# Fewer TensorE instructions in a fused attention and soft-MoE kernel: key pairs turned together, logits computed transposed

## The chip, the core and the metric

The kernel runs on one core of one Trainium2 chip. Five engines work side by side, each with its own queue of instructions: TensorE (PE; its weight loads are shown apart as PEld), VectorE (DVE), ScalarE (ACT), GpSimd (POOL) and SyncE (SP), which here only issues transfers. The metric is the device time of one execution, in microseconds. Three runs of the kernel before gave 298.43, 299.58 and 299.91 us, a median of 299.58.

## The reference

Two layers, one after the other. Attention with a soft cap, over 8 batches of 12 heads, 448 positions and 64 columns a head; its result, 3584 rows of 768, goes into a soft mixture of 8 experts with 4 slots each.

```python
scores = (q @ k.T) / 8
attn = softmax(cap * tanh(scores / cap))        # cap = 30
x = (attn @ v) as rows of 768                   # 12 heads beside each other

logits = x @ phi                                # 3584 x 32
d = softmax of logits over the rows             # dispatch
slot_input = d.T @ x                            # 32 x 768
slot_out[e] = relu(slot_input[e] @ w1[e]) @ w2[e]
c = softmax of logits over the slots            # combine
out = c @ slot_out                              # 3584 x 768
```

## The kernel before

**Quads.** Attention is worked off in 24 quads Q, each of four heads of one batch; three quads are a batch b (`NQB` = 3). Two heads lie side by side in the 128 rows of the array. For a quad, q comes by a casting transfer on GpSimd's queue (`load`, L394) and k by a plain one on SyncE's (`load_k`, L399); VectorE casts k to bf16 (`cast_k`, L403). TensorE turns both (`turn`, L474): 7 tiles of 128 positions times 2 heads, 14 transposes, each with 64 columns of the array, for q as for k. VectorE copies the result to `qT`, `kT` and `km` (`turned`, L480 to L489). The 14 score tiles of a quad go through a ring of PSUM banks (`qk_chunk`, L504 and L507) to ScalarE, which takes the tanh of each chunk (L517) and the exp of 8 tiles at once (L525); the exp of the other 6 is made by VectorE as a sum of four terms (`term`, L532). Then come the products with v (`pv`, L542), the division by the row sum (`norm`, L575 and L576), the turn of x (`x_turn`, L587) and its copy (L591).

**Logits and slots.** After the third quad of a batch, `logits` (L596, L600) multiplies x by phi with x as the weights of the array: 30 matmuls with 32 columns of result each, 128 positions in the partitions. ScalarE takes their exp, `E` (L618, 128 by 128). GpSimd copies the tail rows to `ediag` (L623) and writes `E` four times side by side to `e4` (L628). TensorE adds up `x` times `E` for the slots (`slot_sums`, L671 and L674), sums `e4` with ones for the dispatch's denominators (`e_norm`, L635; `zacc`, L641) and turns `e4` into `ET` (`e_turn`, L646; `e_turned`, L650), the weights of the last product. That is done in the stage for batches 0 to 5; for the last two, turn and copy stand among the output tiles (L990 to L996), and the sum of batch 6 in `z_last` (L805).

**The order.** No scheduler runs on the chip. A class `Plan` lists all steps of the attention stage with engine, duration, dependencies, a due time (`DUE`) and a hold (`HOLD`), plays them through with the durations of `COST`, and the order it gets is written out by hand (`EMIT`) into each engine's queue. Three PSUM banks are handed out by the same plan. The expert weights go along as 56 transfers (`W`): 24 parts of w1, then 32 half parts of w2. Five of the w2 parts stay in SBUF (`KEPT`, `w2b`); 27 are cast from memory to memory (`w2d`, L334).

**The tail.** When the attention's tiles are free, SyncE loads the 27 spilled parts (`w2t`, L859). Then come the last batch's logits and slots, layer 1 (`layer1`, L880), layer 2 (`layer2`, L913, first all parts of the left half of the columns, then all of the right), and 28 output tiles, each `ET` times `so`, scaled and stored (L936 to L1018).

## Time and profile before

| | |
|---|---|
| median of three runs | 299.58 us |
| the profiled execution | 297.8 us |
| its span, first to last instruction | 296.0 us |
| attention, first to last tanh or exp of scores | about 9.6 to 247 us |
| last batch, layer 1 and layer 2 | about 248 to 268 us |
| output tiles and stores | about 263 to 296 us |

A row of the grouped view reads: line, engine, operation, result <- operand, shapes and count, then busy time and mean duration of one in ns, then idle time of the engine just before these instructions and what ended it. "issue" as the releaser means that the engine waited for nothing that another engine or a transfer in the profile did. In a timeline row the two numbers in front are start and length in us, and the idle time before it stands in brackets. In a windows row each engine's busy time in the window stands with its count of instructions in brackets, then the clock granted to TensorE, the share of time in which the 16 DMA engines had packets (queues overlap, so it may exceed 1) and the rate in GB/s. Matmuls overlap: one of 219 ns may start 30 ns after the one before.

### The profile page before, as it was taken

What the parts mean: (1) busy time and instruction counts of PE and PEld (TensorE: products, weight loads), DVE (VectorE), ACT (ScalarE), POOL (GpSimd) and SP (SyncE); (2) the same over time, 40 slices, a digit from 0 to 9 for tenths busy, and PEclk for the clock granted to TensorE, in tenths of its full rate; (3) what the DMA queues carried; (4) which work ended last, traced back from release to release, by engine and by line L of the source; (5) the groups of instructions that cost most, each with busy time, mean ns of one, the idle gap of its engine ahead of it and who ended that gap; (6) DMA issues with size and microseconds to landing.
All of it is one profiled execution on the core that took longest, in us unless ns stands there. A gap on an engine that the chain in (4) does not pass through costs nothing.

```text
span 296.0 us, 11975 instructions
## 1 busy us (share of the span) xinstructions
PE 254.1 (86%) x5300; PEld 186.1 (63%) x5300; DVE 219.7 (74%) x437; ACT 235.1 (79%) x207; POOL 107.6 (36%) x156
## 2 busy tenths in 40 slices
PE   4879999997999898986999998999999989998620
PEld 4348767775777677755767776777777767543300
DVE  2448997995979797866898876998999675246840
ACT  2779999898898899878899997999999994236720
POOL 3652461742652446331536350825343300300000
PEclk9559999999999999999999999999999999999975
DMA  8999999999999999999999999999999989958997
GB/s 159 276 224 242 234 260 235 245 248 230 250 246 237 242 248 247 254 244 223 235 248 232 219 235 241 157 225 245 243 209 228 236 307 346 390 206 310 408 413 306
DMA packets 59075, 75.37 MB, mean 255 GB/s; under 512 B 4880, under 2 KB 48016, under 8 KB 59024
## 3 DMA queue, kind: packets, MB, share of 16 engines
q0 software_dynamic: 30464, 30.50, 62.3%
q1 hardware_dynamic: 28400, 43.89, 46.0%
q8 instruction: 41, 0.67, 0.8%
q10 hardware_dynamic: 160, 0.23, 0.3%
q14 instruction: 10, 0.08, 0.1%
HBM read 94.08 MB, written 21.63 MB: 391 GB/s over the span
## 4 chain that ended last, share of the span: by engine, by line
PE 58%; DMA 15%; DVE 11%; issue 5%; ACT 3%; POOL 2%; SPq 1%; DVEq 0%; ACTq 0%; POOLq 0%
PE pv L542 26%; PE sc L507 9%; DMA qb<-in_q_dram 8%; DMA vraw<-in_v_dram 6%; PE sc L504 3%; PE xps L587 3%; PE qps L474 3%; DVE term L532 2%; PE hp L880 2%; PE so_ps L913 2%; PE kps L474 2%; PE op L1005 2%; DVE kcast L403 1%; DMA raw<-in_q_dram 1%; DVE ob L1012 1%
## 5 line engine op out<-in xcount | busy, mean ns | idle before, releaser
L517 ACT ACTIVATE exa<-sc 128x1344 f16<-128x1344 f32 (+1 forms) x72 | 83.1, 1170 | 21.2 <-PE sc L507 10.9
L525 ACT ACTIVATE exa<-exa 128x3584 bf16<-128x3584 f16 x24 | 76.7, 3197 | 0.0
L517 ACT ACTIVATE exd<-sc 128x896 f16<-128x896 f32 x72 | 64.6, 920 | 0.6 <-PE sc L507 0.5
L542 PEld LDWEIGHTS <-term 128*128 128x128 bf16 x1704 | 55.7, 97 | 12.6 <-issue 8.0
L532 DVE TENSOR_SCALAR term<-exd 128x2688 uint16<-128x2688 f16 (+1 forms) x72 | 61.6, 877 | 1.9 <-PE pv L542 1.2
L507 PE MATMUL sc<-qT,kT 64*128 64x448 bf16 x288 | 53.0, 369 | 2.6 <-ACT exa L517 0.9
L542 PE MATMUL pv<-vb,term 128*128 128x65 bf16 x1136 | 43.6, 193 | 3.0 <-issue 1.7
L414 POOL CAST vb<-vraw 128x1024 bf16<-128x1024 f32 x24 | 26.8, 1117 | 44.3 <-PE pv L542 20.9
L542 PE MATMUL pv<-vb,exa 128*128 128x65 bf16 x960 | 38.7, 193 | 4.1 <-issue 3.3
L542 PEld LDWEIGHTS <-exa 128*128 128x128 bf16 x960 | 33.6, 97 | 10.2 <-issue 7.8
L394 POOL DMA_DIRECT2D qb<-in_q_dram x23 | 18.9, 823 | 53.6 <-PE sc L507 27.8
L576 DVE TENSOR_TENSOR xq<-pv,rec 128x448 bf16<-128x448 f32 (+2 forms) x49 | 30.1, 615 | 1.7
L507 PEld LDWEIGHTS <-kT 64*128 64x128 bf16 x288 | 13.9, 93 | 14.7 <-issue 5.2
L542 PE MATMUL pv<-vw,term 128*128 128x65 bf16 x568 | 22.0, 193 | 1.0 <-issue 1.0
L542 PE MATMUL pv<-vw,exd 128*128 128x65 bf16 x568 | 21.9, 193 | 0.9 <-issue 0.8
L417 DVE TENSOR_SCALAR vw<-vraw 128x512 bf16<-128x512 f32 x24 | 12.3, 512 | 13.1 <-PE pv L542 9.0
L334 POOL DMA_DIRECT2D w2d<-in_moe_w_dram x27 | 21.3, 804 | 1.3 <-issue 0.8
L532 DVE TENSOR_SCALAR exd<-exd 128x2688 uint16<-128x2688 f16 (+1 forms) x24 | 20.4, 850 | 0.8
L542 PEld LDWEIGHTS <-exd 128*128 128x128 bf16 x576 | 19.4, 97 | 1.7 <-issue 1.3
L483 DVE COPY qT<-qps 128x896 bf16<-128x896 bf16 x23 | 14.3, 620 | 8.0 <-PE qps L474 7.8
L628 POOL COPY e<-E 128x512 bf16<-128x512 bf16 x9 | 6.6, 728 | 36.7 <-ACT E L818 18.4
L591 DVE COPY xT<-xps 128x896 bf16<-128x896 bf16 x23 | 14.3, 622 | 7.2 <-PE xps L587 7.0
(135 smaller groups left out, 329.8 us busy)
## 6 DMA issues: line engine op xcount, KB each, us to landing
w1b<-in_moe_w_dram POOLq DMA_DIRECT2D x24, 512.0 KB, 14.7
w2d<-in_moe_w_dram POOLq DMA_DIRECT2D x27, 384.0 KB, 10.8
w2t<-w2d SPq DMA_DIRECT2D x27, 384.0 KB, 5.7
kraw<-in_k_dram SPq DMA_DIRECT2D x23, 448.0 KB, 7.6
out_dram<-ob SPq DMA_DIRECT2D x9, 768.0 KB, 6.8
vraw<-in_v_dram SPq DMA_DIRECT2D x48, 128.0 KB, 7.7
qb<-in_q_dram POOLq DMA_DIRECT2D x23, 224.0 KB, 10.4
vraw<-in_v_dram SPq DMA_DIRECT2D x48, 96.0 KB, 7.6
```

The lines of the kernel that those rows point to most:

```text
L334: pool.dma_start(out=dst, in_=bass.AP(tensor=src.tensor, offset=src.offset + half * HD, ap=[[D, P], [F * D, 4], [1, HD]]))
L394: pool.dma_start(out=t, in_=bass.AP(tensor=srcs[nm].tensor, offset=quad_at(Q), ap=[[NT * DH, P], [2 * S * DH, 2], [1, NT * DH]]))
L414: pool.tensor_copy(vb[Q % 2][:, :, :, 0:DH], vraw[Q % 2])
L474: pe.transpose(ps[h * HP:h * HP + HP, :, x, :], src[:, h, c * DH:(c + 1) * DH], ident)
L483: dve.tensor_copy(new_qkT(nm, Q), ps)
L507: pe.matmul(dst, kT[r, 2 * t:2 * t + 2, :], qT[r], start=True, stop=True)
L517: act.activation(quad_ex(Q, u0, u0 + w).bitcast(F16), ring(Q, s)[:, 0:w, 0:S], ACT.Tanh, scale=qk_scale / cap)
L525: act.activation(t, t.bitcast(F16), ACT.Exp, scale=cap)
L532: dve.tensor_scalar(rows(term_home(Q, i))[:, 0:nd, 0:S].bitcast(U16), quad_ex(Q, NA, NA + nd).bitcast(F16), octaves * 128, base[i], ALU.mu ...
L542: pe.matmul(dst[:, 2 * g + h if g < NF else 2 * g, :], buf[:, q0:q0 + P], vt[:, 3 + h if a is None else 5 * h + t, :], start=begin, stop=e ...
L576: dve.tensor_tensor(xq[Q][:, s0:s1, n, :], ps[:, s0:s1, 0:DH], rec.to_broadcast([P, s1 - s0, DH]), op=ALU.mult)
L591: dve.tensor_copy(xTs[Q], held.pop(("x", Q)))
```

## The change

Keys: the cast writes the two heads of a pair side by side, so that one transpose on the full array turns both; 7 a quad instead of 14. q is turned as before.

Logits: phi, written four times side by side (`phi4`), is the weights of the array and x, turned, streams through it: 6 matmuls of 448 columns a batch. The result has slots in the partitions, four copies of them, and positions in the columns. Its exp, `eT`, gives the dispatch's denominators in the same instruction (`accum_out`), is copied by GpSimd to its place in `ETs` (before: turned), and is turned back by five matmuls to `E` and `ediag` for the slot sums, which VectorE copies out. The last batch keeps the old way.

Memory and order: four w2 parts stay resident instead of five. The plan knows blocks of 256 TensorE instructions and lets a block start no sooner than 6000 ns after the one before; all due times and holds are new. Batch 6's turn, copy and sum leave the tail.

```diff
-DUE = {"C0k": -50327, ...
-HOLD = {"C0k": 688, ...
+PAGE = 256
+COUNT = 179
+DUE = {"C0k": 12624, ...
+HOLD = {"C0k": 1094, ...
...
-                op(("T", nm, Q), "PE", C["turn"], ..., t0, take=True, form=(COLS, COLS))
+                op(("T", nm, Q), "PE", (C["kturn"], C["turn"])[n], ..., t0, take=True,
+                   form=((FULL, FULL), (COLS, COLS))[n], mm=(7, 14)[n])
...
-                op(("EE", b), "ACT", 250, [("LG", b, 1)], tb + 1300, give=("LG", b, 0))
-                op(("ED", b), "POOL", 400, [("EE", b), ("SS", b - 2, 1)], tb + 1600, port=True)
-                op(("SS", b, 0), "PE", 450, [("EE", b)], tb + 2000, take=True)
+                op(("EE", b), "ACT", 500, [("LG", b, 1), ("ER", b - 1), ("ET", b - 1)], tb + 1300, give=("LG", b, 0))
+                op(("ER", b), "POOL", 600, [("EE", b)], tb + 1600, port=True)
+                op(("ET", b), "PE", 320, [("EE", b)], tb + 2000, take=True, mm=5)
+                op(("CE", b), "DVE", 450, [("ET", b), ("SS", b - 1, 1)], tb + 2300, give=("ET", b))
+                op(("SS", b, 0), "PE", 450, [("CE", b)], tb + 3000, take=True, mm=18)
...
-            begin[name], end[name] = t, t + o["dur"]
+            wait, at, n = 0.0, PAGE - count % PAGE, 2 * o["mm"] + (name[0:2] == ("T", "q"))
+            if at <= n:
+                cross = t + o["dur"] * at / n
+                wait = max(0.0, page + COST["page"] - cross)
+                page = cross + wait
+            count += n
+            begin[name], end[name] = t, t + o["dur"] + wait
...
-    KEPT = 5
+    KEPT = 4
...
-        dve.tensor_copy(kcast, kraw[Q % 2])
+        dve.tensor_copy(kcast.rearrange("p c h d -> p h c d"), kraw[Q % 2].rearrange("p h (c d) -> p h c d", d=DH))
...
+            if nm == "k":
+                pe.transpose(ps[:, :, x, :], src[:, TURN[nm][0][x], :, :].rearrange("p h d -> p (h d)"), ident)
+                continue
...
-        for g in range(2 * part, 2 * part + 2):
-            for jt in range(NJ):
-                phi_mms(lps[b][:, g, :], xTs[b * NQB + jt // 2][:, jt % 2, :], g, jt,
-                        jt == 0, jt == NJ - 1)
+        for jt in range(*((0, NJ - 2), (NJ - 2, NJ))[part]):
+            pe.matmul(lps[b], phi4[:, jt, :, :].rearrange("p a s -> p (a s)"), xTs[b * NQB + jt // 2][:, jt % 2, :],
+                      start=(jt == 0), stop=(jt == NJ - 1))
...
-        act.activation(es[b], lps.pop(b), ACT.Exp)
+        act.activation(eT[:, 0:S], lps.pop(b), ACT.Exp, accum_out=zs[b])
+
+    def e_place(b):
+        pool.tensor_copy(ETs[:, b // 2, :, b % 2, :], eT[:, 0:S].rearrange("p (c q) -> p c q", q=HP))
+
+    def e_back(b):
+        ps = held["e", b] = xbank(bank_of["ET", b], [P, NG + 1, NS], name="eps")
+        for g, at in enumerate((0, P, 2 * P, 3 * P, S - P)):
+            pe.matmul(ps[:, g, :], eT[:, at:at + P], ident[:, 0:NS], start=(g == 0), stop=(g == NG), skip_group_check=True)
+
+    def e_backed(b):
+        ps = held.pop(("e", b))
+        es[b] = consts.tile([P, NG, NS], BF16, name="E", tag="E", bufs=1)
+        dve.tensor_copy(es[b][:, 0:NF, :], ps[:, 0:NF, :])
         for h in range(2):
             r = slice(h * HP, h * HP + HP)
-            pool.tensor_copy(ediag[b % 2][r, h, :], es[b][r, NF, :])
+            dve.tensor_copy(ediag[b % 2][r, h, :], ps[r, NF + h, :])
+        if b == 0:
+            dve.tensor_copy(zacc, zs.pop(b))
+        else:
+            dve.tensor_tensor(zacc, zs.pop(b), zacc, op=ALU.add)
...
-    def e_norm(b):
-    def e_normed(b):
...
+        pool.tensor_copy(phi4[:, :, 1:4, :], phi4[:, :, 0:1, :].to_broadcast([P, NJ, 3, NS]))
...
-    z_last(bl - 1)
...
-            e_rep(B - 2)
-        if n == NH + 5:
-            e_turn(B - 2, psT.tile([P, 512], BF16, name="eps", tag="T"))
-            e_turned(B - 2)
```

## The prediction

> **What bounds the kernel now.** I read the page first, then the attention stage in windows, then the waits of ScalarE and of TensorE in that stage, then the timeline around those waits, and last the tail.

> ```profile
> span 296.0 us, 11975 instructions
> PE 254.1 (86%) x5300; PEld 186.1 (63%) x5300; DVE 219.7 (74%) x437; ACT 235.1 (79%) x207; POOL 107.6 (36%) x156
> ...
> q8 instruction: 41, 0.67, 0.8%
> ...
> 20.00:247.00 227.00, 209.41 (x4693) 161.25 (x4694) 188.88 (x364) 207.07 (x169) 95.42 (x118) 1.00 1.15 238
> ...
> L517 ACT ACTIVATE exa<-sc 128x1344 f16<-128x1344 f32 (+1 forms) x69 | 79.7, 1170 | 20.3 <-PE sc L507 10.9 <-PE sc L504 8.9
> ```

> ```profile
> 117.37 0.37 PEld L674 LDWEIGHTS <-xq 128*128 128x128 bf16 x12 [0.95 <-issue]
> ...
> 123.88 0.71 PEld L542 LDWEIGHTS <-term 128*128 128x128 bf16 x21 [0.54 <-issue]
> ...
> 130.33 0.11 PEld L542 LDWEIGHTS <-exa 128*128 128x128 bf16 x2 [1.34 <-issue]
> ...
> 117.36:123.87 6.51, 6.08 (x127) 4.44 (x127) 5.65 (x10) 5.51 (x6) 1.51 (x3) 1.00 1.19 255
> 123.87:130.32 6.45, 5.08 (x128) 4.19 (x127) 5.27 (x12) 5.32 (x4) 4.40 (x5) 1.00 1.24 245
> ...
> sum 38.28, PE 33.68 PEld 26.27 DVE 29.78 ACT 32.72 POOL 13.02; mean PE 5.61 PEld 4.38 DVE 4.96 ACT 5.45 POOL 2.17
> ```

> They do: between one such stall and the next lie 127 or 128 matmuls and 6.45 to 6.51 us, and what TensorE waits for is "issue", nothing that another engine does. The sum row covers six such blocks: 6.38 us each, of which TensorE is busy 5.61. Over the stage, 4693 matmuls are 36.7 blocks in 227 us, 6.19 us a block. TensorE reaches the block's end before the next block has come, time after time. What this costs TensorE, and what else does:

> ```profile
> PE pv L542 <- issue: 6.8, 11, 1.3
> ...
> PE sc L504 <- issue: 1.5, 1, 1.5
> ...
> PE slps L674 <- issue: 0.9, 1, 0.9
> PE qps L474 <- issue: 0.9, 2, 0.7
> ...
> 139.44 0.58 PE L474 MATMUL qps<-ident,qb 128*64 128x128 bf16 x14 [2.03 <-DMA qb<-in_q_dram]
> ...
> 141.45 0.92 ACT L517 ACTIVATE exa<-sc 128x896 f16<-128x896 f32 x1 [2.28 <-PE sc L507]
> ```

> The "issue" rows are 6.8 + 1.5 + 0.9 + 0.9 = 10.1 us in 15 stalls, half of ScalarE's idle time. A late load of q is the other kind: one of them, at 139.44, took 2.28 us from ScalarE.

> [...]

> **The change, part by part.** First the instructions.

> ```profile
> L474 PE MATMUL kps<-ident,kcast 128*64 128x128 bf16 x322 | 14.1, 230 | 0.0
> ...
> L596 PE MATMUL lps<-phib,xT 128*128 128x32 bf16 x126 | 4.5, 176 | 0.0
> L600 PE MATMUL lps<-phib,xT 128*64 128x32 bf16 x84 | 2.6, 186 | 0.0
> L646 PE MATMUL eps<-ident,e 128*128 128x128 bf16 (+1 forms) x32 | 3.7, 214 | 0.0
> ```

> Key turns go from 14 to 7 a quad (322 to 161), logits from 30 to 6 a batch (126 + 84 = 210 to 42), the sum of exps on TensorE goes (24, and 4 at the end), and turning e costs 5 a batch for seven batches and 4 at the end instead of 32: +7. That is 161 + 168 + 28 - 7 = 350 matmuls fewer, 4950 in all, 700 instructions, 2.7 blocks. In the stage it is 7 turns x 22 quads + 168 + 24 + 24 - 35 = 335 of 4693, 7.1%. A block then holds 1/(1 - 0.071) = 1.077 times the work: 5.61 x 0.077 = 0.43 us more. A block that arrives when it does now is reached 0.43 us later, so each of the 15 stalls shrinks by about that: **-6.5 us**. Bounds: 0 (the stalls only move) and -16.2 (every block bound, 2.62 of them at 6.19).

> TensorE's own time hardly changes. Turns, and the logits as they are now:

> ```profile
> 119.80 0.36 PE L504 MATMUL sc<-qT,km 128*128 128x448 bf16 x1
> 120.00 0.55 PE L587 MATMUL xps<-ident,xq 128*128 128x128 bf16 x7
> ...
> 121.92 0.58 PE L474 MATMUL qps<-ident,qb 128*64 128x128 bf16 x14
> ...
> 132.91 0.42 PEld L474 LDWEIGHTS <-kcast 128*64 128x64 bf16 x14 [0.20 <-issue]
> ...
> 133.72 0.33 PE L635 MATMUL zps<-ones,e 128*128 128x1 bf16 x4
> ...
> 143.72 0.60 PE L596 MATMUL lps<-phib,xT 128*128 128x32 bf16 x18
> 144.25 0.36 PE L600 MATMUL lps<-phib,xT 128*64 128x32 bf16 x12
> ```

> Seven full transposes (0.55, the x turn) cost what 14 half ones do (0.58). A full matmul of 448 columns lets the next one start after 0.20 (119.80 to 120.00), so six logits take about 1.2 us where they take 0.89 now (143.72 to 144.61): +0.3 x 7. Against it stand the four sums (0.33) and four turns of e (3.7 us for 32, 0.46 for four), six times, for five turns in their place at that price (0.58): -0.2 x 6. I take 0 for the two together, bounds -1.2 and +2.1. Before the half-array turns TensorE waits 0.20 us of "issue", which I take for the switch of the array's shape; a full turn next to other full work saves it. 23 turns: -4.6 at most, 0 if the neighbours are score matmuls on half the rows, as they often are. I take **-1.0**.

> ScalarE and VectorE:

> ```profile
> L517 ACT ACTIVATE exa<-sc 128x1344 f16<-128x1344 f32 x48 | 62.2, 1295 | 10.2 <-PE sc L504 9.8
> L517 ACT ACTIVATE exa<-sc 128x896 f16<-128x896 f32 x24 | 22.1, 919 | 11.0 <-PE sc L507 10.9
> ...
> L618 ACT ACTIVATE E<-lps 128x128 bf16<-128x128 f32 x7 | 2.0, 282 | 0.0
> ...
> L403 DVE CAST kcast<-kraw x23: 616/627/1605, 11.5 to 224.8; 128x896 bf16<-128x896 f32 x23
> ...
> L417 DVE TENSOR_SCALAR vw<-vraw x24: 417/425/947, 18.1 to 235.3; 128x512 bf16<-128x512 f32 x24
> ...
> L650 DVE COPY ET<-eps 128x448 bf16<-128x448 bf16 x6 | 2.4, 392 | 0.2
> ...
> L623 POOL COPY ed<-E 64x32 bf16<-64x32 bf16 x14 | 7.0, 498 | 22.8 <-ACT E L618 22.4
> ```

> The exp of the logits grows from 128 to 448 columns. From 1295 and 919 ns a column costs 0.84 ns over a base of 167: 543 instead of 282 ns, 0.26 x 7 = **+1.8 us**, all on the bound engine. The sum that comes with it has no row; bounds 0 and a second small operation of 282 ns (+2.0); I take 0. Behind this exp the next tanh queues on ScalarE, so lateness of the logits is paid there.

> The key cast now writes pieces of 64. The nearest row is the vw cast, which writes pieces of 64 too: 425 ns for 512, 0.83 a column against 0.70 for the packed cast; so 627 becomes 740, +0.11 x 23 = 2.6 us of VectorE. Bounds 0 and double (1254 ns, +14.4). The evacuation of e, now the copy of 392 ns and a small add, becomes four operations on 32 to 96 columns and one of them that add; at half of that copy for each it is 0.78 in place of 0.59, +0.2 x 7 = 1.4. VectorE is idle 38 of the 227 us (the window row), which hides most of the 4.0; I take **+0.5**, bounds 0 and +4.0, the latter if a quad's turn waits for all of it; without the fast form of the cast +14.4 more.

> GpSimd loses the 14 small copies, 7.0 us, and makes seven copies of 448 columns in place of seven of 512. Its first copy waits for the same exp on ScalarE as now (22.4 us in all), and the others behind it. v's cast, q's loads and the weights queue behind them; **-1.0**, bounds 0 and -7. The new wait, the back turn behind the exp, stands in place of the slot sums' present wait for the same exp and holds TensorE's queue alike: 0.

> The fifth resident w2 part becomes a transfer of the tail:

> ```profile
> L913 PE MATMUL so_ps<-w2t,hpad x108: 326/326/337, 259.8 to 267.8; 128*32 128x384 bf16 x108
> ...
> 253.86 2.30 SPq L859 DMA_DIRECT2D w2t<-w2d  x3
> ...
> DMA to landing us min/median/max: 3.0/5.7/7.8
> ...
> 264.00:270.00 6.00, 4.96 (x68) 1.99 (x68) 4.18 (x8) 2.32 (x4) 0.00 (x0) 1.00 0.63 218
> 270.00:280.00 10.00, 8.19 (x51) 3.94 (x50) 8.52 (x13) 7.72 (x10) 0.61 (x1) 1.00 1.02 390
> ```

> The last part is asked for before 256.2, lands some 5.7 us later, at 262, and is used near 267: 5 us of cover for 384 KB, which at 390 GB/s is 1.0 us. Cost 0, +1.0 without the cover. From 270 the stores bound the tail (share 1.02), so the turn and copy removed there give nothing.

> Three smaller moves cost nothing: phi's four copies are made once on GpSimd, which is busy 95.4 of the stage's 227 us; e's last replication goes behind the clearing of hpad, and its reader comes only among the output tiles; the sum of batch 6's exps leaves the end, where TensorE runs it while a copy of x is made.

> Moving all the due times is a new order of every queue, each load of q, k, v and w2 included. Nothing in this trace prices it; I take 0 and bound it by the q load at 139.44, below.

> **Sum:** -6.5 - 1.0 + 0 + 1.8 + 0.5 - 1.0 = -6.2 us. The profiled execution took 297.8 us (span 296.0 and 1.8 around it), so 291.6; the median, 299.58, lies 1.8 above it, so I forecast **293.4 us** for the median.

> **The rivals.** (1) Every block was bound, not 15 of 37: -16.2 and the same other terms, -15.9, inside what ScalarE leaves (19.9 less 1.8). For it: 6.19 us a block over the whole stage is what the stalled blocks show. Against: a block still needs TensorE's 6.04 us. Between half and all of it, 284 to 292; **288**. (2) The transfers bind: all stage long the DMA share is 1.15, and a faster TensorE only waits longer for q and v. For it the wait at 139.44; against it the share of 0.63 to 1.0 after the weights are in. The gain goes: **299**. (3) Slower: q's loads. In GpSimd's new order a load of q falls behind one more weight part, and the quad's turn waits, as at 139.44, 2.28 us of ScalarE. With three such loads more the gain of 6.2 is gone; five cost 11.4: **304.8**. (4) The blocks aren't what TensorE waits for, so the change doesn't give what fewer instructions should: only +1.8 + 0.5 remain, **301.9**.

> **How the numbers follow.** Forecast 0.46, rivals 0.18, 0.12, 0.18, 0.06. Forecast and first rival are faster; with a part of the second, 0.66. Same, within 0.5% (1.5 us, about what a measurement of this kernel can tell from no change), 0.08; the rest, 0.26, is slower. The forecast's own range is 289 to 297 (double gain on the blocks, or none with -1.0 kept). The range that should hold 8 in 10 takes in most of the first rival and reaches to just under the third: 286 to 304.

> **What would show it.** TensorE with some 4950 matmuls and 38 instruction packets; its "issue" stalls still 128 matmuls apart, with 10.1 us shrunk to 3 or 4; ScalarE's 20.3 us ahead of exa shrunk by about as much; the logits' exp near 540 ns; the key cast near 740; GpSimd's small copies gone; the window after 264 as now. Wrong would be a stage as long as now with the "issue" stalls gone (rival 2), stalls as large as now (rival 4), or more rows like that of 139.44 (rival 3).

## The result and the profile after

The change made the kernel slightly slower: 300.37 us, median of 13 runs (299.37 to 303.08), against 299.09 of 13 runs of before beside them (297.39 to 301.05), ratio 1.0059 [1.0032, 1.0085]. Forecast was 293.4. The profiled execution after took 301.7 us, its span is 299.9 against 296.0. Medians here and below are of all runs, while ratios leave out runs more than 1.5% above the fastest of the same kernel, which matters for one kernel below, the change in the old order, with five of ten left out.

The instructions are as forecast. From the page of after:

```profile
span 299.9 us, 11307 instructions
PE 255.7 (85%) x4950; PEld 183.3 (61%) x4950; DVE 228.6 (76%) x452; ACT 237.4 (79%) x214; POOL 102.9 (34%) x143
...
q8 instruction: 39, 0.64, 0.8%
```

Exactly 4950 matmuls, and 39 packets on the instruction queue instead of 41. What TensorE waited for between 20 and 247 us, in the view of waits of after (total, times, longest in us):

```profile
PE pv L552 <- DVE term L542: 4.7, 4, 2.3
PE pv L552 <- ACT exa L535: 3.2, 6, 0.7
PE kps L480 <- DVE kcast L410: 2.8, 1, 2.8
PE pv L552 <- issue: 2.2, 5, 0.6
PE slps L689 <- DVE qT L493: 1.2, 1, 1.2
...
PE qps L484 <- DMA qb<-in_q_dram: 0.6, 1, 0.6
...
PE xps L597 <- issue: 0.4, 1, 0.4
```

The stalls of "issue" went from 10.1 us to 2.6, a little more than the forecast's 6.5 less. In their place stand waits for VectorE that before hardly had, the longest 1.8 to 2.8 us each, and behind two of them TensorE's clock fell to half. From the windows view of after (columns as before, the clock is the third number from the right):

```profile
40.90:44.30 3.40, 3.40 (x41) 2.56 (x38) 2.82 (x8) 1.61 (x2) 1.07 (x2) 0.50 1.12 245
...
112.60:116.00 3.40, 2.75 (x48) 2.67 (x49) 2.93 (x6) 2.02 (x2) 0.84 (x1) 0.50 1.16 242
```

and from TensorE's timeline of after, the waits ahead of them:

```profile
39.33 0.91 PE L552 MATMUL pv<-vw,term 128*128 128x65 bf16 x24 [1.78 <-DVE term L542]
...
113.25 1.50 PE L552 MATMUL pv<-vw,term 128*128 128x65 bf16 x24 [2.35 <-DVE term L542]
```

At half clock 24 products with v took 1.50 us, not 0.91. The one at 113.25 goes back to a load, as VectorE's timeline of after shows: the cast of a quad's keys stands ahead of the terms in VectorE's queue, and it waited for its transfer.

```profile
111.49 0.77 DVE L410 CAST kcast<-kraw 128x896 bf16<-128x896 f32 x1 [2.44 <-DMA kraw<-in_k_dram]
112.17 1.02 DVE L542 TENSOR_SCALAR term<-exd 128x2688 uint16<-128x2688 f16 x1
```

Where the time went is seen best from when ScalarE starts the large exp of a quad (L525 before, L535 after, start times in the timeline):

| start of the exp of quad | 0 | 1 | 3 | 10 | 13 | 23 | span |
|---|---|---|---|---|---|---|---|
| before, us | 15.00 | 25.50 | 43.81 | 113.12 | 145.77 | 242.07 | 296.0 |
| after, us | 16.34 | 29.33 | 51.68 | 123.36 | 151.32 | 244.66 | 299.9 |

From quad 13 on the change gains: 93.3 us for ten quads instead of 96.3. Up to quad 13 it loses 5.55 us: 1.34 before quad 0's exp and 9.66 in quads 1, 3 and 10 (12.99, 13.27 and 12.74 us; 9 to 10.5 before), of which the other quads win back 5.45. The tail loses another 1.3 us: the last w2 load is issued at 262.6 us instead of 255.8, and layer 2 waits for it. From TensorE's timeline of after:

```profile
270.33 0.35 PE L920 MATMUL so_ps<-w2t,hpad 128*32 128x384 bf16 x4 [0.61 <-DMA w2t<-w2d]
```

So fewer instructions did shorten the "issue" stalls, and the gain was taken back. Two things could do that: the new order, or loads that do not come sooner than they did. The view of transfers of before, between 100 and 150 us (issues, KB each, median us from issue to landing), holds the second, and the prediction did not read it:

```profile
w2d<-in_moe_w_dram POOLq DMA_DIRECT2D x12, 384.0 KB, 17.8
kraw<-in_k_dram SPq DMA_DIRECT2D x5, 448.0 KB, 7.6
...
qb<-in_q_dram POOLq DMA_DIRECT2D x4, 224.0 KB, 16.6
```

A load of q shares its queue with the weights and lands 16.6 us after its issue. If that is what holds it, a TensorE that arrives sooner only waits longer for it; groups 1 and 3 below test this.

### The profile page after: what moved, and what is told of

Read it like the earlier page. It is cut to its first block, busy times and chain, and to the rows that moved or that the text cites. A ratio compares the mean times of both kernels' runs of the same rounds, so it can differ in the third digit from the quotient of the medians.

```text
span 299.9 us, 11307 instructions
## 1 busy us (share of the span) xinstructions
PE 255.7 (85%) x4950; PEld 183.3 (61%) x4950; DVE 228.6 (76%) x452; ACT 237.4 (79%) x214; POOL 102.9 (34%) x143
## 4 chain that ended last, share of the span: by engine, by line
PE 41%; DMA 21%; ACT 16%; DVE 11%; issue 4%; POOL 2%; SPq 1%; DVEq 0%; ACTq 0%; POOLq 0%
PE pv L552 21%; DMA kraw<-in_k_dram 9%; ACT exa L535 8%; PE sc L517 7%; DMA w2t<-w2d 6%; ACT exd L527 5%; DMA vraw<-in_v_dram 4%; PE sc L514 3%; DVE term L542 3%; PE xps L597 2%; PE kps L480 2%; DMA raw<-in_q_dram 2%; PE qps L484 2%; PE lps L621 1%; ACT ob L1017 1%
## 5 line engine op out<-in xcount | busy, mean ns | idle before, releaser
L527 ACT ACTIVATE exa<-sc 128x1344 f16<-128x1344 f32 (+1 forms) x72 | 82.0, 1176 | 16.2 <-PE sc L514 13.6
L535 ACT ACTIVATE exa<-exa 128x3584 bf16<-128x3584 f16 x24 | 76.7, 3196 | 0.0
L542 DVE TENSOR_SCALAR term<-exd 128x2688 uint16<-128x2688 f16 (+1 forms) x72 | 62.4, 884 | 8.8 <-ACT exd L527 4.9
L552 PEld LDWEIGHTS <-term 128*128 128x128 bf16 x1704 | 58.4, 98 | 15.5 <-DVE term L542 7.0
L517 PE MATMUL sc<-qT,kT 64*128 64x448 bf16 x288 | 51.2, 371 | 2.1 <-ACT exa L527 1.2
L552 PEld LDWEIGHTS <-exa 128*128 128x128 bf16 x960 | 34.4, 99 | 11.8 <-ACT exa L535 7.3
L341 POOL DMA_DIRECT2D w2d<-in_moe_w_dram x28 | 23.2, 855 | 0.0
L517 PEld LDWEIGHTS <-kT 64*128 64x128 bf16 x288 | 13.3, 93 | 14.8 <-issue 7.0
L542 DVE TENSOR_SCALAR exd<-exd 128x2688 uint16<-128x2688 f16 (+1 forms) x24 | 20.7, 862 | 0.8
L410 DVE CAST kcast<-kraw 128x896 bf16<-128x896 f32 x23 | 18.1, 787 | 3.7 <-DMA kraw<-in_k_dram 3.3
L337 POOL DMA_DIRECT2D w1b<-in_moe_w_dram x24 | 18.3, 765 | 0.0
L514 PE MATMUL sc<-qT,km 128*128 128x448 bf16 x48 | 18.2, 379 | 0.0
L424 DVE TENSOR_SCALAR vw<-vraw 128x512 bf16<-128x512 f32 x24 | 11.5, 480 | 8.5 <-PE pv L552 7.4
```

The source lines that it names most:

```text
L337: pool.dma_start(out=w1b[e][:, js, :], in_=w1r[:, e, js, :])
L341: pool.dma_start(out=dst, in_=bass.AP(tensor=src.tensor, offset=src.offset + half * HD, ap=[[D, P], [F * D, 4], [1, HD]]))
L410: dve.tensor_copy(kcast.rearrange("p c h d -> p h c d"), kraw[Q % 2].rearrange("p h (c d) -> p h c d", d=DH))
L514: pe.matmul(dst, km[Q % 2][:, n, :], qT, start=True, stop=True)
L517: pe.matmul(dst, kT[r, 2 * t:2 * t + 2, :], qT[r], start=True, stop=True)
L527: act.activation(quad_ex(Q, u0, u0 + w).bitcast(F16), ring(Q, s)[:, 0:w, 0:S], ACT.Tanh, scale=qk_scale / cap)
```

## The experiments

Letters of theories in the expectations hold within one group of runs. Ratios are against runs of before on the same chip, with 95% intervals.

**1. Each part alone, and the whole change in the old order.** The keys' part is the diff's two edits of L403 and L474 in before. The other two runs are the changed kernel, with old keys and with new ones, whose plan is given the begin times of before's plan, so that every engine keeps before's order:

```diff
+BEFORE = {("CA", "k"): 0, ("L", "q", 1): 0, ...
+            o["due"], o["hold"] = BEFORE[o["name"]], 0
-strict = ("ACT", "DMA")
+strict = engines
```

> The kernel before, in its own order, with only the keys changed: interleaving cast, 7 full transposes a quad. 161 matmuls fewer. Theory A (the new order of the queues costs what fewer instructions save): 161 of 350 matmuls of the 6.5 us, so 3 us faster, ratio 0.990, and the issue rows of TensorE in the stage shrink from 10.1 us to about 7. Theory B (the transfers bind, fewer instructions give nothing): ratio 1.00 with smaller issue rows, the time going to waits for loads. Theory C (the transposed logits' longer chain from the exp to the slot sums costs the time): like A here, 0.990.

> The changed kernel with the keys as before, and with the steps in the order of the kernel before (its planned begin times, kept on every engine; the back turn and its copy 0.9 and 1.5 us behind the exp of the logits, the placing copy where the small copies stood). Four resident w2 parts. 189 matmuls fewer. Theory A: 3.5 us less, 1.8 us more on ScalarE: ratio 0.993. Theory B: 1.00 to 1.01. Theory C: slower, 1.01 or more, with ScalarE or TensorE waiting seven times between exp, back turn and slot sums.

> The whole change, but with the steps in the order of the kernel before on every engine (as in the run with the logits alone). Theory A: what the steps were forecast to give, 5 to 7 us faster than before, ratio 0.977 to 0.985, and no wait of TensorE for VectorE of over 2 us. Theory B: 1.00. Theory C: 1.00 or more, and slower than the keys alone by 2 us or more.

Measured: keys alone 297.72 us, 0.9939 [0.9905, 0.9974]; logits alone 299.79, 1.0021 [0.9983, 1.0058]; both in the old order 303.23, 1.0071 [1.0011, 1.0130] (298.8 and 298.9 in two runs, as long as before, and 302.1 to 303.9 in the other eight; 1.014 by the medians). All three lie above what theory A gave for them, and the new order is thus not needed for the loss. In the old order the longest wait is q's, and the clock falls behind it. TensorE's timeline of this run, profiled in one of the eight, and a window of it:

```profile
141.00 0.96 PE L488 MATMUL qps<-ident,qb 128*64 128x128 bf16 x14 [4.52 <-DMA qb<-in_q_dram]
141.89 1.94 PE L556 MATMUL pv<-vb,exa 128*128 128x65 bf16 x32
```

```profile
141.00:146.40 5.40, 5.40 (x66) 3.91 (x66) 3.23 (x6) 0.92 (x1) 1.46 (x2) 0.50 1.27 220
```

That is the load of 139.44 in the prediction: issued at 122.8 us it landed at 139.4 there, and issued at 124.1 it landed at 141.0 here, although TensorE asked for it 0.9 us sooner. The wait grew from 2.03 to 4.52 us, and then the 5.4 us of this window ran at half clock. The quad of that wait took 16.75 us, 11.79 in before; that difference of 5.0 is as much as this run is behind at quad 13 (150.53 against 145.77). Quad 7 took 14.59 us instead of 10.58, behind a load of v that VectorE waited for, and the other quads made that good. At quad 23 the run is only 1.7 us behind; 3.5 more of its span are lost in the tail, behind this stall:

```profile
252.77 0.20 PE L610 MATMUL lpl<-phi,xT 128*128 128x32 bf16 x2 [1.49 <-issue]
```

Group 5 comes back to it.

**2. Two moves that mend what the changed kernel's profile shows.** In its own order two casts of keys were moved on VectorE: quad 2's (with a scaling of v) ahead of the first term, and quad 12's, with the load that follows it, to just ahead of the copy of E of batch 2:

```diff
+    ahead([("KC", 2), ("VS", 0)], ("PH", 0, 0))
+    ahead([("KC", 12), ("LK", 14)], ("CE", 2))
```

> The changed kernel with two places of its order mended: quad 2's key cast and quad 0's scaled v go ahead of the first term of quad 0 on VectorE, as they stood before, and quad 12's key cast and the load behind it go 10 places back, behind the terms of quad 9. Theory A: quads 1 and 10 take 10 us from exp to exp in place of 13.0 and 12.7, 5 us less in all: ratio to the kernel before 0.988. Theories B and C: those waits turn up elsewhere, 1.005 as the change.

Measured: 300.71 us, 1.0056 [1.0030, 1.0083]. The two quads were mended (1: 10.35 us, 10: 9.48), but quads 3 and 12 now took 14.85 and 12.12, and the exp of quad 13 started at 152.04, no sooner than in the changed kernel. The waits turned up elsewhere, as theories B and C had it. Mending these two waits one by one gave nothing; the run doesn't show what sets quad 13's time.

**3. The loads relieved.** First by spacing alone: the plan hands out the 56 weight transfers evenly by number, though the first 24 (w1) are 512 KB and the others 384. The spaced version issues the same bytes in proportion to time, without any other engine's order changed. Then by leaving out the w1 parts of every second expert.

```diff
             t = 3000 + k * (NQ * T - T) / self.parts
+            t = BEFORE["W", k]
```

> The whole change in the order of the kernel before (the run e3_old_order), with one thing moved: the 56 weight transfers are spread over the same time by their bytes (512 KB for a w1 part, 384 for a w2 part) and not by their number, so that some four parts fewer stand ahead of the loads of q up to quad 13. Theory B (up to quad 13 the transfers bind: weight parts queue up ahead of q and v, and a faster TensorE only meets late loads): the wait for q of 4.5 us and the one of 3.6 us for VectorE's term shrink below 2 us, quad 13's exp starts before 147 us (150.5 in e3_old_order), ratio to before 0.98 to 0.99. Theory A (the order alone): no change, 1.007. Theory D (the loads are late because GpSimd issues them late, not because parts stand ahead): no change either.

> The kernel before, its order kept on every engine, with the weight transfers spread by bytes as in e5_old_order_paced. Theory B: TensorE stays short of instructions, so only its waits for loads go (2 to 3 us): ratio 0.990 to 0.995, and the issue rows of 10 us stay. Theories A and D: 1.00.

> The kernel before without the w1 transfers of every second expert (the neighbour's w1 is used in layer 1): 12 of 24 parts and 6 MB less in the first half of the stage. Theory B: q lands in 5 us or so, waits for q go, the issue rows stay near 10 us: 296, ratio 0.99. Theories A and D: 1.00.

> The whole change in the order of the kernel before, without the w1 transfers of every second expert (the neighbour's w1 is used in layer 1). Theory B: with the transfers out of the way fewer instructions give what was forecast, so 6 us less than the run e7_before_half_w1: 290, ratio to before 0.97; no wait of TensorE for q over 1 us up to quad 13. Theory A: the forecast gain came with the old order already or not at all: equal to e3_old_order, 1.007. Theory C (the longer chain behind the logits costs the time): 2 us or more slower than e7_before_half_w1.

Measured: the change so spaced 294.92 us, 0.9848 [0.9823, 0.9872]; before so spaced 298.43, 0.9956 [0.9920, 0.9992]; with half of w1, before 289.89, 0.9711 [0.9652, 0.9770], and the change 290.12, 0.9691 [0.9669, 0.9714]. Moving transfers alone takes 2.2% off the changed kernel in the old order and 0.4% off before. In the old order it is thus the places of the weights among the loads that take the gain. It isn't less traffic: from 60 to 100 us the change in the old order, first as it was and then spaced, shows nearly the same rate and the same share of the 16 DMA engines, while TensorE gets more done:

```profile
60.00:100.00 40.00, 35.58 (x727) 27.11 (x724) 32.81 (x67) 35.03 (x31) 17.47 (x21) 0.96 1.13 243
```

```profile
60.00:100.00 40.00, 37.54 (x795) 28.35 (x794) 34.20 (x71) 37.54 (x32) 16.40 (x19) 1.00 1.13 246
```

q lands in before so spaced in 5.9 us (the view of transfers, same window):

```profile
qb<-in_q_dram POOLq DMA_DIRECT2D x4, 224.0 KB, 5.9
```

Yet before gains only 0.4% by it. Its waits for q are gone, and its "issue" stalls grew from 10.1 to 14.0 us, of which most are (20 to 247 us):

```profile
PE pv L547 <- issue: 9.8, 14, 1.6
```

So with loads on time it is the instruction blocks that TensorE waits for (14.0 us of "issue" in before so spaced), and with fewer instructions it is the loads (4.52 us for one load of q in the old order). Spacing alone gave 0.4%, the change alone cost 0.7%, and the two together gave 1.5%.

With half of w1 left out, before took 289.89 us where 296 was expected. The change met its 290, but by luck: it was to be 6 us faster than before so run, and it is no faster. "Issue" falls by itself there, from 10.1 to 7.6 us (20 to 247 us), and 128 matmuls take 5.93 us in before (6.19 with all of w1, mean of 30 to 240 us), so less is left to gain; but the change brought "issue" to 3.7 us, and the exp of quad 23 still starts at 234.4 us in before and at 234.2 in the change. ScalarE works 201.3 and 203.6 of the 214 us from 20 to 234 in these two runs. Its added work, some 3 us (below), may take the rest; no run tests that.

**4. Parts and order once the loads are on time.** The keys' part spaced; the whole change in its own order spaced; before with four resident w2 parts; the logits' part spaced.

> The keys' part alone in the order of before, with the 56 weight transfers spaced by their bytes. Theory A (the weights' backlog takes back what the shorter instruction stream saves): keys alone were 0.994 of before, the spacing alone 0.996, and together they bring more than the two in a row, 0.985 to 0.988 (about 295 us), since q is no longer late for a faster TensorE; waits for q's load below 1 us in all. Theory B (the two have nothing to do with each other): 0.9895 (about 296 us). Against the whole change in the same order and spacing (0.985): if this run is below it, the logits' part costs time even in relieved traffic, if it is above, the logits' part gains.

> The whole change in its own order, only the places of the 56 weight transfers on GpSimd moved to an even spacing by bytes. If the transfers are what took the gain and the order of the engines is not: about 0.985 of before (295 us), as the old order with this spacing, quads 3 and 10 below 10.5 us. If the new order costs by itself (k's cast placed ahead of the terms on VectorE, which waits in order): 0.992 to 1.000 (297 to 299 us), with quad 1 still above 12 us and waits of 2 to 3 us for VectorE's term left on TensorE.

> Before with four resident w2 parts instead of five and nothing else. Predicted at 0, since the last w2 part lay 5 us ahead of its use: 0.998 to 1.002. The rival, that one part more written to memory and read back in the tail is felt: the last w2 loads land late, TensorE waits for w2t at layer 2, 0.6 to 1.3 us, 1.002 to 1.004.

> The logits' part alone (with four resident w2 parts, which by themselves were 0.999) in the order of before, with the weight transfers spaced by bytes. So spaced, before was 0.996, the keys' part 0.979 and the whole change 0.985. If the logits' part costs ScalarE and TensorE time that no transfer excuses (its exp of 0.53 us and the wait for it): 0.998 to 1.004. If its 196 instructions fewer are worth what the keys' 336 were per instruction once q is on time (0.979/0.996, so 1.7% for 336): 0.986 to 0.988. In between: the instructions gain and the exp gives it back, 0.992 to 0.997.

Measured: keys 293.32 us, 0.9788 [0.9732, 0.9843], more than keys and spacing in a row (0.9895); own order 297.17, 0.9935 [0.9903, 0.9967]; four resident parts 298.43, 0.9991 [0.9962, 1.0020], nothing; logits 292.84, 0.9770 [0.9731, 0.9809], where the part alone had given nothing unspaced. The logits' part came out below all that was expected for it. The instructions in that expectation are miscounted: the keys' part has 161 matmuls fewer and the logits' part 189, so 322 and 378 instructions, not 336 and 196; at the keys' price 378 are worth 2.0%, which gives 0.976, near the 0.977 that was measured. The own order costs 0.9%, about 2.6 us, against the old order with the same spacing. At the exp of quad 23 it is 5.6 us behind (239.88 against 234.31); the whole times differ by less because the old order's tail holds the stall of group 5. Spacing shortened its quads 3 and 10, to 11.73 and 10.82 us, but its quad 1 still takes 13.17 us. From TensorE's waits in that run:

```profile
PE kps L485 <- DVE kcast L415: 2.9, 1, 2.9
```

That wait is the order's: the first move of group 2 took it away with the weights unspaced. But each part alone (0.979, 0.977) beat both together (0.985), though the attention of both together ends sooner (exp of quad 23 at 239.0, 236.8 and 234.3 us).

**5. Where the edge of a block falls.** In the spaced change in the old order the lost time is at the attention's end. TensorE's timeline, and a window behind it:

```profile
243.27 0.20 PE L611 MATMUL lpl<-phi,xT 128*128 128x32 bf16 x2 [1.49 <-issue]
...
248.14 5.36 PE L892 MATMUL hp<-w1b,slT 128*32 128x512 bf16 x72
```

```profile
243.00:250.00 7.00, 6.73 (x102) 4.06 (x105) 1.01 (x5) 1.03 (x3) 2.36 (x2) 0.57 1.03 402
```

An instruction block came 1.49 us late amid matmuls that are short anyway, and the clock was at half from 243.9 to 250.8 us, into the middle of layer 1's first 72 matmuls. From the exp of quad 23 to the end this run takes 58.5 us, before 54.0. In before the stalls lie 127 or 128 matmuls or a multiple apart; if the place of the edges is thus set by the number of instructions ahead, the warming matmuls at the start, which write nothing that is used, move all of them:

```diff
-    busy(29, junk, by=nc.const_aps.tensor(1.0, [P, P], BF16))
+    busy(5, junk, by=nc.const_aps.tensor(1.0, [P, P], BF16))
```

> The whole change in the order of before with the weights spaced by bytes (0.985), and 24 of the 29 warming matmuls at the start left out, which write nothing that is used: each block of 256 TensorE instructions then ends 48 instructions later in the program. If what the two parts together lose against either alone (0.985 against 0.979 and 0.977) is the place where the edge of a block falls at the end of the attention (1.49 us of issue at L611 at 241.8 us, and half the clock from 243 to 250): the stall shrinks to below 0.8 us, layer 1's first 72 matmuls take 4.1 us instead of 5.4, and the time is 0.973 to 0.979 (291 to 293 us). If it is something else (28 loads of w2 parts in the tail, the copies of the logits): 0.983 to 0.987, with the stall gone or not.

> The same with 32 warming matmuls more at the start instead (61), so that each block ends 64 instructions earlier. The start may take up to 2 us more if the first scores wait for the warming matmuls, none if these end before the first cast does at 6 us. If the edge's place is what counts: the stall falls in the last products with v near 239 us, where 0.5 to 1.5 us of it remain, and the clock then stays full through layer 1 since no second wait follows it; 0.974 to 0.981. If it is something else: 0.983 to 0.990.

Measured: 290.12 us, 0.9704 [0.9665, 0.9743], and with 61 instead of 29 matmuls 290.90, 0.9709 [0.9680, 0.9737]. The stall is gone and layer 1 runs at full clock. The edges moved as counted: 128 matmuls behind the stall of 1.49 us are 46 matmuls into layer 1, and with 32 warming matmuls more a wait of 0.22 us for "issue" stands 14 into it. The same window of the run with 5 warming matmuls, and its matmuls of layer 1:

```profile
241.00:248.00 7.00, 6.94 (x154) 4.59 (x154) 2.16 (x10) 1.03 (x3) 2.37 (x2) 1.00 1.03 396
```

```profile
246.00 4.28 PE L892 MATMUL hp<-w1b,slT 128*32 128x512 bf16 x72
```

72 of them in 4.28 us instead of 5.36. From the exp of quad 23, which starts at 234.59 us instead of 234.31, to the end it takes 53.7 us instead of 58.5, so the whole gain of the moved edges lies in the tail. This is the best version found, 3% below before. The same step in before, in the changed kernel and in before spaced:

> Before with 24 of its 29 warming matmuls left out, which write nothing that is used, and nothing else: every block of 256 TensorE instructions ends 48 instructions later in the program. If the place of the edges gave the whole change with spaced weights its 1.5% (0.985 to 0.970) and every program has such a chance in it, before moves too, by 0.5 to 1.5% in one direction. If before's attention is bound by the fetch of blocks and by q's loads wherever the edges lie: 0.996 to 1.004, the sum of its issue stalls still 9 to 12 us between 20 and 247 us.

> The changed kernel as it is (own order, weights spaced by number), with 24 of its 29 warming matmuls left out. If an unlucky edge is what made the change slow: 0.985 to 0.992. If the loads' backlog and the order are: 1.000 to 1.008, with quads 1, 3 and 10 again over 12 us and VectorE's term and kcast waits of 2 to 3 us on TensorE.

> Before with the weights spaced by bytes (0.996) and the same 24 warming matmuls left out: what the spacing and the edges bring without any of the change. If the whole change is worth its instructions once q is on time: 0.990 to 1.000 here against its 0.970. If the spacing and the edges explain nearly all and the change little: 0.970 to 0.978.

Measured: 299.37 us, 1.0024 [0.9993, 1.0056]; 301.53, 1.0082 [1.0047, 1.0116]; 296.82, 0.9916 [0.9882, 0.9950]. The edges do not explain the loss of the changed kernel; of the best one's 3.0% they give half. With weights spaced and the same 24 warming matmuls left out, the change in the old order takes 290.12 us against 296.82, **6.7 us** or 2.3% (2.1% by the two ratios, each against its own runs of before). With all 29 it is 294.92 against 298.43, 3.5 us.

That difference is the stall in the tail: at the exp of quad 23 the change is 8.2 us ahead with 29 (234.31 against 242.56) and 7.8 with 5 (234.59 against 242.36). The main runs beside each other, one trace each (q: median us from issue to landing, 100 to 150 us; exps start in us):

| | ratio | q lands | exp of quad 13 | of quad 23 | span |
|---|---|---|---|---|---|
| before | 1 | 16.6 | 145.77 | 242.07 | 296.0 |
| the change | 1.006 | 12.3 | 151.32 | 244.66 | 299.9 |
| change, old order | 1.007 | 16.9 | 150.53 | 243.81 | 301.3 |
| before, spaced | 0.996 | 5.9 | 146.15 | 242.56 | 296.2 |
| before, spaced, edges moved | 0.992 | 6.0 | 145.48 | 242.36 | 295.9 |
| change, own order, spaced | 0.994 | 9.4 | 146.42 | 239.88 | 295.8 |
| change, old order, spaced | 0.985 | 11.2 | 139.39 | 234.31 | 292.9 |
| the same, edges moved | 0.970 | 10.5 | 140.53 | 234.59 | 288.3 |
| before, half of w1 | 0.971 | 6.4 | 140.27 | 234.42 | 288.1 |

## Why the prediction was wrong

**Right: the instructions.** 350 matmuls are gone and the stalls of "issue" are shorter by 7.5 us, against 6.5 forecast; part of that may be the new waits, which leave blocks more time to come. Spaced and in the old order the change is worth 6.7 us with 5 warming matmuls and 3.5 with 29. That 6.7 is near the -6.2 of the sum is partly luck: the keys' part alone, spaced, took 1.7% off before so spaced and the logits' part 1.9%, together more than the whole, and with half of w1 left out the change gave nothing. That TensorE does wait at the blocks' ends is in before's rows: at 15 of some 37 in the stage, 127 or 128 matmuls or a multiple apart, 10.1 us in all.

**The step that failed** is the sum itself, in two terms that were put at 0. One is the order. "Moving all the due times is a new order of every queue ... Nothing in this trace prices it; I take 0": with spaced weights the new order costs 2.6 us in all, and 5.6 us at the exp of quad 23. The other is the loads. The -6.5 was taken as time off the end, as if q, k and v came when TensorE asks; in the old order, spacing the weights alone moved (one trace each) the exp of quad 23 from 243.81 to 234.31 us, where before stays at 242. The two don't add up: with the weights unspaced the new order is only 0.9 us behind the old one at that exp.

The loads were the second rival (the transfers bind, 299), given 0.12 because of the share of 0.63 to 1.0 after the weights are in. That share belongs to the tail; it says nothing of the time up to quad 13, in which the weights stand among the loads and the loss arises. The view of transfers in that time, with 16.6 us for a load of q, spoke for this rival. The fourth rival (301.9) is near in time too, but it needs "issue" stalls that the change doesn't shorten, and they fell from 10.1 to 2.6 us.

**The rival's price was too small.** It put a late load at what TensorE waits and so at no worse than no gain. In the old order the wait for q grew by 2.5 us (2.03 to 4.52), and with the half clock behind it its quad took 5.0 us longer, so that a faster TensorE comes out slower. The third rival had the right sign by another place: in the changed kernel TensorE waited for q only 0.6 us in all, and for VectorE's terms and casts 7.5.

**The smaller terms.** The logits' exp takes 542 ns against 543 forecast; its sum is an instruction of its own and takes 1.4 us in all, where 0 was forecast (bounds 0 and 2.0). ScalarE's groups of after in the stage:

```profile
L631 ACT ACTIVATE eT<-lps 128x448 bf16<-128x448 f32 x7 | 3.8, 542 | 1.0 <-PE lps L621 0.4
L631 ACT ACTIVATION_READ_ACCUMULATOR eT<-lps 128x1 f32 x7 | 1.4, 197 | 0.0
```

The key cast takes 659 ns in the median, not 740 (627 before): the vw cast was the wrong row to go by. Instead VectorE's small add of the denominators took 764 to 1476 ns, after 159 in before; that is 6.8 us in all (the six durations), 6.0 more than before had for it, with the rest of VectorE's queue behind it. The prediction had priced it at half of a copy, 196 ns. For the cast it names the double of 627 as a bound, without the cast's fast form: that was its author's assumption, and single casts took up to 1570 ns in after and 1605 in before. The views of the cast's line and of this tile in after (min/median/max in ns, then first and last start):

```profile
L410 DVE CAST kcast<-kraw x23: 616/659/1570, 13.2 to 223.3; 128x896 bf16<-128x896 f32 x23
```

```profile
L652 DVE TENSOR_TENSOR zacc<-zb,zacc x6: 764/1066/1476, 91.9 to 235.6; 128x1 f32<-128x1 f32 x6
```

GpSimd's timeline shows what the add is likely to wait for. A cast of v runs there during all six, and each add ends within 0.03 us of the end of that cast. The second of the six, VectorE's row and then GpSimd's:

```profile
123.21 1.47 DVE L652 TENSOR_TENSOR zacc<-zb,zacc 128x1 f32<-128x1 f32 x1
```

```profile
123.53 1.13 POOL L421 CAST vb<-vraw 128x1024 bf16<-128x1024 f32 x1
```

In the old order, unspaced, two of the six adds have no such cast beside them and take 160 ns; the other four take 857 to 868.

The 28th spilled part was rightly put at 0 (0.9991 alone); in the new order the loads of all spilled parts come late, and the 0.61 us above is that order's. The saving of 1.0 at the switch of the array's shape and GpSimd's 1.0 were not measured by themselves; ahead of the key turns' weight loads "issue" stands for 4.4 us in before (21 waits) and 3.7 in after (15).

One reading in the prediction is off and changes nothing here: its range of 289 to 297 doesn't follow from its words; double the gain on the blocks gives 286.9, and none of it 299.9.

**Open.** Moved edges bring 1.5% in one version, by its tail, and nothing in before or in the changed kernel, whose tails were not so long (54.0 and 55.2 us from the exp of quad 23, against 58.5). Which edge will hurt is not shown beyond the one stall that was traced. In the changed kernel quad 1's loss is the order's, since a move on VectorE mended it and spacing did not; quad 3's was not divided. Spacing moves the weights among the loads of q, k and v alike: how much of its gain is q's, which shares their queue, and how much that of k and v, which come by another, was not separated. And why the change brings nothing with half of w1 left out is not shown.

## What to carry to other kernels

A stall removed is time gained only up to the next thing that comes at its own time: here 7.5 us of "issue" went, and the median rose by 1.3. Before pricing a faster engine, read from issue to landing of each load that it will ask for sooner, in the stage where it asks, and whether its queue holds bulk transfers that could come later. And price a wait of TensorE with the half clock that may follow it: through one such wait, two parts that each gained 2% gave 1.5% together.

## What the runs showed of the hardware

In the changed kernel TensorE's clock stood at half for 3.41 us from 40.90 us on and again from 112.58, behind waits of 1.78 and 2.35 us; in the 3.41 us ahead of each fall TensorE was busy for 1.63 and 1.73. In the change in the old order, spaced, it stood at half for 6.9 us behind a wait of 1.49. A small add on VectorE took up to 1.48 us instead of 0.16 and ended with a cast that GpSimd ran at the same time. And a load of q landed 16.6 us after its issue among weights issued evenly by number, and 5.9 with the same weights spaced by bytes (before, 100 to 150 us).
